# Dealing the late y rows from SBUF with one copy per bank, moves on two queues, and every store on Sync

## The chip, the cores and the metric

The kernel runs on one core of a Trainium2 chip. The metric is the device time of one execution in microseconds (us), as the median of several runs. A ratio is the mean time of one kernel's fast runs over the mean time of the other's fast runs of the same rounds, so it is not quite the ratio of the medians quoted beside it; each ratio comes with a 95% interval. "Faster" or "slower" is said only from 2% on, which is 8.8 us here.

In the profile PE is TensorE's matmul side, DVE is VectorE, ACT is ScalarE, POOL is GpSimd and SP is Sync; "SPq" and "ACTq" are the sequencers of Sync and ScalarE, where transfers are issued. L1005 is line 1005 of the kernel's text.

## The reference, cut to what matters

Attention with a forget gate over `q, k, v, f` of (8, 8, 576, 64) gives `x` of (8, 576, 512). Then a spectral mix is added and a layer closes it:

```python
X = np.fft.rfft(x, axis=1)[:, :64]                 # 64 modes
Y[:, :64] = X * (w_r + 1j * w_i)                   # a 512x512 matrix for each mode
u = x + np.fft.irfft(Y, n=576, axis=1)
out = u + np.maximum(u @ w_ch, 0.0)
```

## The kernel before

The weights of the 64 modes stream in for most of the time. When the last modes are done, their results ("the late y rows", 16 rows of each of the 8 batches) must be put into the tile `yy`, from which the inverse transform reads. They come out of PE in two PSUM banks: `ply` (transposed y, bf16) and `plw` (y times `w_ch`, f32). Batch 0's rows are copied to `yy` directly. The other batches' rows lie in other partitions, so a bank is first emptied into `yl` in SBUF, and then DMA transfers ("moves", 16 KB each) carry them:

```python
y_rows(YTl, 0, ply[:, :], plw[:, :])                                  # PE fills both banks
nc.vector.tensor_copy(row_slot(0, 0, H2, H4), ply[0:H4, :])           # batch 0 straight from PSUM
nc.scalar.copy(yls[0][:, 0, :], ply[:, :])                            # the whole bank, by ScalarE
emit_moves(yls[0], H2, 1, 0, nc.gpsimd)
run(terms(jobs[0], ps, 0, "y"))
nc.vector.tensor_copy(row_slot(0, 1, H2, H4), plw[0:H4, :])
nc.vector.tensor_copy(yls[0][:, 1, :], plw[:, :])
emit_moves(yls[0], H2, 1, 1, nc.gpsimd)
for b in range(2, B):
    for t in range(2):
        emit_moves(yls[0], H2, b, t, nc.gpsimd)
```

Then 20 jobs make the output. Jobs 0 to 3 and 4 belong to batches 0 and 1, jobs 5 to 9 to batches 2 and 3, and so on. In each, PE fills two PSUM tiles: `pu` (u) and `pz` (u @ w_ch). ScalarE copies `pu` to SBUF, VectorE combines `pz` with it, and the result is stored:

```python
def emit_u(job, ps, u, split=False):
    ...
        nc.scalar.copy(u[:, bs, :], ps[0][:, bs, :])

def emit_o(job, ps, u, o, pair, split=False):
    ...
        nc.vector.scalar_tensor_tensor(
            o[:, bs, :], ps[1][:, bs, :], 0.0, u[:, bs, :], ALU.max, ALU.add
        )
        if sb == 4:                                # the last 64 rows of two batches
            for h in range(2):
                eng = nc.scalar if job is jobs[-1] and h else nc.sync
                eng.dma_start(out[b + h, 512:576, :], o[64 * h : 64 * h + 64, 0, :])
        ...                                        # all other stores: nc.sync.dma_start
```

The very last job's output leaves as two half-stores (64 partitions, 128 KB each): one on Sync, one on ScalarE.

The softmax here doesn't subtract the row's maximum and nothing guards it: scores larger than these inputs give would overflow.

## Time and profile before

| | before |
|---|---|
| median of the first three runs | 437.82 us (437.63 to 437.91) |
| profiled span | 435.5 us |
| first `ply` transpose, where the changed code begins | 401.68 us |
| VectorE's last combination ends | 427.82 us |
| last store has landed | 434.2 us |
| ScalarE's queue (q10) | 80 packets, 0.13 MB |
| Pool's issues in the tail | 14 moves |

The table reads as three stretches: 401.7 us that the change does not touch, 26.1 us from the late rows to VectorE's end, and 7.7 us of draining stores and closing. The lines that show the limits of each are in the prediction. The same cut, with all times counted from the start of the `ply` transposes, is used for every kernel below, because the moment at which that start comes differs between the traces by up to 1.8 us (400.5 to 402.2), as the result will show.

### The profile page before, as it was taken

Reading aid. Unit: us, or ns where it says so; the run is one execution under the profiler, and the core shown is the slowest. Engines: PE = TensorE matmul, PEld = TensorE weight load, DVE = VectorE, ACT = ScalarE, POOL = GpSimd, SP = SyncE. Lnnn points to the kernel's source line nnn. Section 1 sums busy time; section 2 is a strip of 40 time slices with the busy share of each in tenths; the row PEclk is TensorE's granted clock in tenths of the full one; section 3 lists DMA queues with packets and bytes.
Section 4 is the critical chain, followed back from the end, with each engine's and each line's share of the span. In section 5 each row is a group of like instructions: output and inputs, shape, how many; then the busy total and the mean of one; then the engine's idle time right before and its main releaser. Section 6 shows DMA issues by size and latency. Waiting matters only on the chain.

```text
span 435.5 us, 12294 instructions
## 1 busy us (share of the span) xinstructions
PE 361.2 (83%) x5295; PEld 245.6 (56%) x5313; DVE 264.0 (61%) x658; ACT 224.8 (52%) x340; POOL 128.6 (30%) x202
## 2 busy tenths in 40 slices
PE   3787799999987977778768797799999978989981
PEld 2353666676665655666556565666665544644440
DVE  5797788876465655546656577524324653743892
ACT  2887488774626356364364554143443442731771
POOL 7333332333233233232333222233223223200600
PEclk9997699996557668557587779599999998989997
DMA  8999999999999999999999999999999999994698
GB/s 182 234 235 240 235 236 239 235 212 237 233 215 237 225 224 237 211 236 230 216 237 212 211 211 211 212 211 211 211 211 211 211 211 211 211 211 97 225 374 293
DMA packets 50981, 97.37 MB, mean 224 GB/s; under 512 B 3792, under 2 KB 12976, under 8 KB 50928
## 3 DMA queue, kind: packets, MB, share of 16 engines
q0 software_dynamic: 46688, 86.16, 100.9%
q1 hardware_dynamic: 4160, 10.31, 6.5%
q8 instruction: 41, 0.67, 0.6%
q10 hardware_dynamic: 80, 0.13, 0.2%
q14 instruction: 12, 0.10, 0.1%
HBM read 163.73 MB, written 9.44 MB: 398 GB/s over the span
## 4 chain that ended last, share of the span: by engine, by line
PE 39%; DMA 23%; ACT 12%; DVE 10%; issue 4%; POOL 0%; DVEq 0%; ACTq 0%
DMA wb<-in_moe_w_i_dram 22%; ACT E L576 8%; PE pav L614 8%; PE A L188 7%; PE ps L569 7%; PE tp L307 5%; PE px L657 3%; DVE QTs L322 2%; PE vp L541 2%; PE pu L828 2%; ACT KT L320 2%; PE pz L828 1%; DVE XT L671 1%; DVE os L1005 1%; DVE E L591 1%
## 5 line engine op out<-in xcount | busy, mean ns | idle before, releaser
L576 ACT ACTIVATE E<-ps 128x1024 bf16<-128x1024 f32 (+1 forms) x128 | 101.5, 851 | 24.0 <-PE ps L569 13.4
L93 POOL DMA_DIRECT2D wb<-in_moe_w_r_dram x64 | 42.5, 664 | 124.8 <-PE A L188 25.0
L188 PE MATMUL A<-XT,wb 128*128 128x16 bf16 x1984 | 69.9, 181 | 10.5 <-DMA wb<-in_moe_w_i_dram 5.7
L188 PEld LDWEIGHTS <-wb 128*128 128x128 bf16 x1984 | 63.4, 100 | 24.9 <-issue 12.1
L569 PE MATMUL ps<-QTs,KT 64*128 64x64 bf16 (+4 forms) x384 | 58.2, 322 | 19.9 <-ACT E L576 17.9
L93 POOL DMA_DIRECT2D wb<-in_moe_w_i_dram x64 | 42.3, 660 | 80.7 <-DMA wb<-in_moe_w_i_dram 36.8
L614 PE MATMUL pav<-va,E 128*128 128x65 bf16 (+1 forms) x1088 | 55.2, 209 | 3.1 <-DVE x_all L636 2.6
L614 PEld LDWEIGHTS <-E 128*128 128x128 bf16 (+1 forms) x1088 | 45.3, 114 | 18.7 <-issue 9.1
L591 DVE TENSOR_TENSOR E<-E,trimask 128x256 bf16<-128x256 bf16 (+2 forms) x128 | 37.0, 303 | 20.3 <-ACT E L576 20.0
L326 ACT COPY VT<-tp 128x640 bf16<-128x640 bf16 (+1 forms) x32 | 23.2, 761 | 34.0 <-PE tp L307 34.0
L867 ACT CAST XW<-pxw 128x512 bf16<-128x512 f32 x36 | 20.7, 586 | 35.7 <-PE pxw L860 23.5
L569 PEld LDWEIGHTS <-KT 64*128 64x128 bf16 x384 | 19.1, 98 | 33.1 <-issue 21.7
L320 ACT COPY KT<-tp 128x640 bf16<-128x640 bf16 (+1 forms) x32 | 22.0, 750 | 26.4 <-PE tp L307 26.2
L910 ACT CAST XW<-pB 128x512 bf16<-128x512 f32 x36 | 20.9, 585 | 28.1 <-PE pB L828 28.0
L860 PE MATMUL pxw<-wch,yy 128*128 128x512 bf16 x133 | 33.6, 385 | 1.2 <-issue 0.7
L909 DVE CAST x_all<-pA 128x512 bf16<-128x512 f32 x36 | 24.9, 692 | 15.2 <-PE pA L828 13.4
L322 DVE COPY QTs<-tp 128x640 bf16<-128x640 bf16 (+1 forms) x32 | 23.3, 768 | 13.9 <-PE tp L307 13.7
L636 DVE TENSOR_TENSOR x_all<-pav,rcp 128x384 bf16<-128x384 f32 x64 | 29.2, 456 | 0.9
L625 DVE RECIPROCAL rcp<-pav 128x6 f32<-128x6 f32 x64 | 12.1, 190 | 24.1 <-PE pav L614 23.4
L153 DVE TENSOR_TENSOR YTe<-A,Yacc 128x128 bf16<-128x128 f32 x16 | 5.9, 368 | 33.1 <-PE A L188 33.1
L828 PEld LDWEIGHTS <-ident_bf 64*64 64x64 bf16 (+1 forms) x348 | 15.7, 109 | 17.6 <-issue 8.8
L541 PE MATMUL vp<-ident_bf,VT 128*128 128x128 bf16 x160 | 17.1, 247 | 5.2 <-DVE QTs L322 4.6
(143 smaller groups left out, 620.0 us busy)
## 6 DMA issues: line engine op xcount, KB each, us to landing
wb<-in_moe_w_r_dram POOLq DMA_DIRECT2D x62, 512.0 KB, 17.0
wb<-in_moe_w_i_dram POOLq DMA_DIRECT2D x62, 512.0 KB, 17.6
stv<-in_v_dram POOLq DMA_DIRECT2D x10, 576.0 KB, 15.2
out_dram<-os SPq DMA_DIRECT2D x10, 512.0 KB, 4.8
stk<-in_k_dram POOLq DMA_DIRECT2D x11, 288.0 KB, 15.2
stq<-in_q_dram POOLq DMA_DIRECT2D x11, 288.0 KB, 15.2
wx<-in_v_dram POOLq DMA_DIRECT2D x5, 576.0 KB, 15.5
out_dram<-uo SPq DMA_DIRECT2D x3, 512.0 KB, 4.3
```

The lines of the kernel that those rows point to most:

```text
L93: keep(nc.gpsimd.dma_start(dst, src))
L188: ins = nc.tensor.matmul(A[:, eb, mi, :], lhsT=w_of(mi, eb * 128), rhs=x_of(m), start=(i == 0), stop=(i == len(terms) - 1),)
L320: nc.scalar.copy(rows(KTs[pr % 2][:, :, 0:S]), tv)
L322: ins = nc.vector.tensor_copy(rows(QT[pr][:, :, :]), tv)
L541: nc.tensor.transpose(vp[:, sc, :, :].rearrange("p b d -> p (b d)"), VTs[s // 2 % 2][:, h, sc * 128 : (sc + 1) * 128], ident_bf[:, :],)
L569: nc.tensor.matmul(ps[:, b, o : o + n], lhsT=KTs[pr % 2][bs, h, jb * 128 : (jb + 1) * 128], rhs=QT[pr][bs, h, jb * 128 + c0 : jb * 128 + c ...
L576: nc.scalar.activation(E[:, :, piece * 512 : piece * 512 + w], ps[:, :, 0:w], ACT.Exp, scale=scale,)
L591: nc.vector.tensor_tensor(dg, dg, tr, ALU.mult)
L614: nc.tensor.matmul(pav[64 * half : 64 * half + w, slot, :], lhsT=E[:, b, c : c + (w - 1) * st + 1 : st], rhs=va[:, jb, b, :], start=(n == ...
L636: nc.vector.tensor_tensor(xo, pi, ri, ALU.mult)
L828: return nc.tensor.matmul(p, lhsT=lhsT, rhs=rhs, start=first, stop=not first, skip_group_check=True)
L860: nc.tensor.matmul(pxw[:, :], lhsT=xT[:, eb, i * 128 : (i + 1) * 128], rhs=wch[:, eb, :], start=(eb == 0), stop=(eb == NDC - 1),)
```

## The change

Its intent: ScalarE is freed of one copy and PSUM of double reading; each late bank is read once, by VectorE, and batch 0 is dealt from SBUF; the moves of batches 1 and 2 go out on Sync, the others on Pool, so that batches 3 and 4 wait less; the last half-store moves from ScalarE to Sync. The diff in full:

```diff
--- before.py
+++ after.py
@@ -821,7 +821,7 @@
         def emit_moves(yl, r0, b, t, eng):
             p0 = H4 * b
             ins = eng.dma_start(row_slot(b, t, r0, H4), yl[p0 : p0 + H4, t, :])
-            if eng is nc.gpsimd:
+            if eng is nc.gpsimd or r0 == H2:
                 tc.keep_in_program_order(ins)
 
         def add(p, lhsT, rhs, first):
@@ -1009,8 +1009,7 @@
                 n_wide = 4 * (b // 2 - 1) + sb
                 if sb == 4:
                     for h in range(2):
-                        eng = nc.scalar if job is jobs[-1] and h else nc.sync
-                        eng.dma_start(
+                        nc.sync.dma_start(
                             out[b + h, 512:576, :], o[64 * h : 64 * h + 64, 0, :]
                         )
                 elif not wide(job):
@@ -1066,14 +1065,18 @@
         ply = ply[:, 0 : D // 2].bitcast(BF16)
         plw = psL.tile([128, D], F32, tag="A", name="plw")
         y_rows(YTl, 0, ply[:, :], plw[:, :])
-        nc.vector.tensor_copy(row_slot(0, 0, H2, H4), ply[0:H4, :])
-        nc.scalar.copy(yls[0][:, 0, :], ply[:, :])
-        emit_moves(yls[0], H2, 1, 0, nc.gpsimd)
+        def late_rows(t, src):
+            keep(nc.vector.tensor_copy(yls[0][:, t, :], src))
+            keep(nc.vector.tensor_copy(row_slot(0, t, H2, H4), yls[0][0:H4, t, :]))
+            for b in (1, 2):
+                emit_moves(yls[0], H2, b, t, nc.sync)
+            for b in (3, 4):
+                emit_moves(yls[0], H2, b, t, nc.gpsimd)
+
+        late_rows(0, ply[:, :])
         run(terms(jobs[0], ps, 0, "y"))
-        nc.vector.tensor_copy(row_slot(0, 1, H2, H4), plw[0:H4, :])
-        nc.vector.tensor_copy(yls[0][:, 1, :], plw[:, :])
-        emit_moves(yls[0], H2, 1, 1, nc.gpsimd)
-        for b in range(2, B):
+        late_rows(1, plw[:, :])
+        for b in range(5, B):
             for t in range(2):
                 emit_moves(yls[0], H2, b, t, nc.gpsimd)
         lctx.close()
```

The pin (`keep_in_program_order`) also covers the moves of Sync. PE's stream is the same in both kernels; only copies, moves and the last store change their place.

## The prediction

> **What bounds the kernel now.** I read the page first, for the stages; then the chain that ended last, for the stretch that the change touches; then the timeline there; last the table by stretches, for what limits the end. From the page:
>
> ```profile
> PE   3787799999987977778768797799999978989981
> ...
> DMA  8999999999999999999999999999999999994698
> GB/s 182 234 235 240 235 236 239 235 212 237 233 215 237 225 224 237 211 236 230 216 237 212 211 211 211 212 211 211 211 211 211 211 211 211 211 211 97 225 374 293
> ```
>
> One slice is 10.9 us. For 36 of 40 slices the DMA engines are full (the weights arrive). The change touches none of that: all its lines run after the last mode tile, so 401 of the 435.5 us stand. Only the last 34 us are in play: first the late y rows are dealt to their places, then 20 jobs are computed (PE fills two PSUM tiles, ScalarE copies one, VectorE combines both) and stored. The chain in order of time, around the dealing:
>
> ```profile
> 401.70 0.38 PE ply L809 x4
> ...
> 404.68 1.43 POOL yy L823 x3
> 406.12 3.42 DMA yy<-yl
> 409.53 0.04 issue
> 409.57 0.40 PE pu L828 x2
> ```
>
> This is the wait that the change is after. Pool issues 14 moves of 16 KB; the fifth is the first half of batch 3, issued at 406.12, landing 3.42 us later, and PE has to hold job 5 (batches 2 and 3) for it. The timeline of the engines (start, us, engine, line, what; in brackets the idle time before and what ended it) shows how much that costs:
>
> ```profile
> 402.12 0.41 DVE L1069 COPY yy<-ply 16x512 bf16<-16x512 bf16 x1 [0.49 <-PE ply L809]
> 402.57 0.58 ACT L1070 COPY yl<-ply 128x512 bf16<-128x512 bf16 x1 [7.46 <-DVE yy L1069]
> ...
> 402.98 0.68 DVE L1073 CAST yy<-plw 16x512 bf16<-16x512 f32 x1 [0.45 <-PE plw L813]
> ...
> 403.70 0.69 DVE L1074 CAST yl<-plw 128x512 bf16<-128x512 f32 x1
> ...
> 404.51 1.29 DVE L1005 SCALAR_TENSOR_TENSOR uo<-pz,uo 128x512 f32<-128x512 f32 x2
> ...
> 404.68 4.77 POOL L823 DMA_DIRECT2D yy<-yl  x10 [0.43 <-DVE yl L1074]
> ...
> 409.57 0.40 PE L828 MATMUL pu<-yy,BIl 64*64 64x512 bf16 x2 [0.39 <-DMA yy<-yl]
> ...
> 410.48 0.69 DVE L1005 SCALAR_TENSOR_TENSOR uo<-pz,uo 128x512 f32<-128x512 f32 x1 [0.40 <-PE pz L828]
> ```
>
> PE loses 0.39 us to the move, and VectorE then 0.40 us before job 4 at 410.48, where its other breaks are about 0.2 us. So the wait on show is small. The last view is the busy time by stretches:
>
> ```profile
> 410.00:414.00 4.00, 3.73 (x59) 2.04 (x58) 3.57 (x5) 3.57 (x4) 1.04 (x3) 1.00 0.93 336
> 414.00:418.00 4.00, 3.63 (x59) 1.91 (x54) 3.64 (x4) 3.00 (x5) 0.00 (x0) 1.00 1.02 383
> ...
> 422.00:426.00 4.00, 3.54 (x56) 1.75 (x49) 3.60 (x4) 2.94 (x3) 0.00 (x0) 1.00 1.03 405
> 426.00:430.00 4.00, 0.69 (x6) 0.13 (x3) 1.83 (x3) 0.58 (x1) 0.00 (x0) 0.95 1.01 387
> ```
>
> The last two numbers of a line are the DMA share and GB/s. VectorE is busy 3.6 of each 4 us, and from 414 on the DMA engines are full with stores. The tail is bound by both; VectorE ends at 427.82, the last store lands at about 434.2. An earlier start of the jobs moves both; a wait removed that is shorter than VectorE's own work moves nothing.
>
> **What the Trainium skill says.** "PSUM — Partial Sum Buffer", Terms: two engines may not be at the same bank and quadrants at once, reads included. The trace agrees: ScalarE's copy of ply starts at 402.57, 0.04 us after VectorE's copy from the same bank ends (402.12 + 0.41). "VectorE: DVE Perf Modes", The perf-mode tier table: a bf16 copy runs at up to 4x from SBUF, at most 2x from PSUM. The trace agrees: 128x512 bf16 from PSUM took 416 ns (0.81 ns per element), 128x1152 bf16 from SBUF 461 ns (0.40). "DMA: Bandwidth & Descriptors", Issuing engines are not separate DMA queues: transfers from all issuers share the 16 DMA engines, so another issuer saves only issue time. The trace agrees so far as one queue, Sync's, alone fills them from 414 to 429.
>
> **The change part by part.**
>
> (1) VectorE's work. Before: 16x512 from PSUM (0.41), 16x512 cast (0.68), 128x512 cast (0.69): 1.78 us. After: 128x512 bf16 from PSUM (0.42, as the like copy of yl from yp), 128x512 cast (0.69), and two 16x512 copies within SBUF. For these the nearest rows are 64x640 at 0.32 and 128x64 at 0.26, so I estimate 0.30 each. Sum 1.71: the same. ScalarE loses one copy of 0.58, while it was otherwise waiting for PE (its next copy starts at 403.54 on PE's word), so nothing is won there.
>
> (2) When batch 0 can go on. Its first half was in place at 402.53, now at 402.53 + 0.04 + 0.30 = 402.87. PE is in the plw matmuls until 402.87 anyway: cost under 0.1. Its second half was in place at 403.66; now 402.98 + 0.69 + 0.30 = 403.97, so 0.3 later. The last matmuls of job 0 started at 403.72 right on that copy, so VectorE's first combination slips from 404.51 to about 404.8. Against that, the plw bank is read for the last time at 403.67 instead of 404.39, and job 1's second PSUM tile, which reuses it, waited until 404.44 for that. PE may thus do job 1 as early as before, and VectorE, which stood 0.22 us idle before job 1, reaches it at 406.0 to 406.1 against 406.02. Net +0.05 for jobs 1 to 3.
>
> (3) The moves. On Sync, batches 1 and 2, first half: ready 402.53, issued at 402.6 and 403.2 (0.59 each in the trace), second half at 403.7 and 404.3, done by 405. Sync's earlier moves end at 401.23 and its first store begins at 405.23, so the stores do not queue behind them. Pool: batch 3 at about 402.9 instead of 406.12, and 403.9 for its other half. With 3.5 us to land, the median of both queues, batch 3 is in place at 406.4 and 407.4, some 2 us before PE asks at 409.0. The wait of 0.39 goes wholly. VectorE's job 4 then starts at 410.1 to 410.2 instead of 410.48, job 5 at about 410.85 instead of 411.09 (it also needs a PSUM tile free from job 3, which ends at 410.1). Gain 0.25 after the 0.05 of part 2.
>
> (4) The moves also leave the DMA engines before 410 rather than at 413.6. Pool's queue took 5.5% of the engines from 400 to 420, which is 1.1 us for 14 moves, 0.08 us each; the four or so that fell after 410 are 0.3 us of work in the nearly full stretch. But stores were still limited by VectorE there; I count nothing.
>
> (5) The last stores. Before, one half went out on ScalarE at 427.86 and landed in 4.8 us; the other on Sync at 428.99, because Sync was held to 428.90 by the store ahead, took 1.42 to issue and landed 5.2 us later, at 434.2: it sets the end. Now both are on Sync, so the second is issued at about 430.4 less what is gained. The earlier pair of such stores, at 422.97 and 424.16, landed 0.33 apart, the second 4.0 us after its issue. So: the first lands 0.3 us sooner, as 128 KB less (0.3 us at 405 GB/s) share the engines, the second 0.33 after it, at 434.2 to 434.4. Cost 0.05.
>
> Sum: -0.25 (parts 2 and 3) + 0.05 (part 5) = -0.2 us. 437.82 - 0.2 = 437.6.
>
> **The rivals.** First, *the end becomes an issue chain on Sync*. If the second half-store lands 4.7 us after its issue (the median of all half-stores) and not 4.0, the end is 435.1, 0.9 us later, and the gain of part 3 only takes it back to +0.65: 438.5. For it speaks that Sync's half-stores took 1.1 to 1.6 us to issue under load; against it, that the engines are full until 433.3, so the second store's bytes queue behind others anyhow. Second, *the start binds*: the 0.3 us by which batch 0's second half is late runs through PE, VectorE and all jobs, with the bank's early release worth nothing since job 1's next matmuls also wait for a ScalarE copy ending at 404.61. That makes part 3 only cancel it: 437.9. Third, *the moves were worth more than the one wait shows*: the tail's jobs close up, the store stream starts full 0.5 us sooner, and the end follows: 437.2. Fourth, *the dealt rows are hidden anyway*: the DMA engines bound the end whatever VectorE does, and the time does not move, 437.8.
>
> **Range and chances.** Every path stays within 1 us, and 2% is 8.8 us; even all 34 us of the tail would have to shrink by a quarter. The three runs before span 0.28 us, so another build adds 0.2 or so. Predicted 437.6 us, range 437.0 to 438.3. Faster by over 2%: 0.01; within 2%: 0.98; slower by over 2%: 0.01.
>
> **What would show it.** Part 1: two 16x512 copies within SBUF near 0.30 us; a row near 0.4 or more makes part 2 worse. Part 2: VectorE's first combination at about 404.8 and job 1 near 406.0; if job 1 starts at 406.3, the second rival holds. Part 3: no wait of PE for a move, batch 3 issued by Pool near 402.9, and job 4 on VectorE by 410.2. Part 5: the interval between the last two landings, and the time from VectorE's end to the end of the span, 7.7 us before. It would be wrong if the compiled order of the matmuls around job 0 and 1 changed, if Pool took over a microsecond to wake, or if Sync's moves were slowed so that the first stores start after 405.6.

## The result, and the profile after

| | before | after |
|---|---|---|
| median, 6 runs each | 437.73 us (437.27 to 438.17) | 436.77 us (435.82 to 437.33) |
| ratio | | 0.9975, 95% interval 0.9961 to 0.9988 |
| profiled span | 435.5 us | 435.2 us |

"Same" at 2%, as foreseen, but the gain is 0.96 us and not 0.2, and the median lies 0.23 us below the predicted range. All outputs are right. The page after, its two rows on the DMA engines, 40 slices of the span:

```profile
DMA  8999999999999999999999999999999999995797
GB/s 184 234 235 241 234 236 238 235 212 236 234 215 236 225 224 237 210 238 233 214 237 211 212 211 212 211 211 211 211 211 211 212 210 211 211 211 100 253 367 274
```

They answer to the rows that the prediction shows: full until the tail, then a dip while the rows are dealt, then stores. Nothing there tells 1 us. VectorE around the dealing, after (start, us, engine, line, what; in brackets the idle time before it and what ended it):

```profile
401.35 0.42 DVE L1069 COPY yl<-ply 128x512 bf16<-128x512 bf16 x1 [0.49 <-PE ply L809]
401.81 0.28 DVE L1070 COPY yy<-yl 16x512 bf16<-16x512 bf16 x1
402.21 0.69 DVE L1069 CAST yl<-plw 128x512 bf16<-128x512 f32 x1
402.94 0.29 DVE L1070 COPY yy<-yl 16x512 bf16<-16x512 bf16 x1
403.99 2.52 DVE L1005 SCALAR_TENSOR_TENSOR uo<-pz,uo 128x512 f32<-128x512 f32 x3 [0.77 <-DMA yy<-yl]
...
410.48 1.23 DVE L1005 SCALAR_TENSOR_TENSOR os<-pz,us 128x1024 f32<-128x1024 f32 x1 [0.54 <-issue]
```

The small copies take 0.28 and 0.29 us. The moves go out as planned; Sync's and Pool's issues in the same kernel:

```profile
401.80 2.41 SPq L823 DMA_DIRECT2D yy<-yl  x4
```

```profile
402.47 4.81 POOL L823 DMA_DIRECT2D yy<-yl  x10 [17.17 <-DVE yy L1070]
```

The chain of waits after no longer holds a move: it runs from the last weights through PE to VectorE's jobs (with one store among them, from 416.86 to 420.50), and no piece of Pool is in it.

Two profiles can't be subtracted as they stand. The `ply` transposes start at 401.68 us before and at 400.91 after, 0.77 us apart, though no line ahead of them has changed. The stretch from 384 to 390 us shows where this comes from (busy time of PE, its weight loads, VectorE, ScalarE and Pool, then the granted clock, which is the share of TensorE's full clock that the chip allowed, the DMA share and GB/s), first before, then after:

```profile
384.00:390.00 6.00, 5.56 (x59) 2.92 (x60) 2.22 (x4) 1.42 (x3) 0.53 (x1) 0.72 1.12 211
```

```profile
384.00:390.00 6.00, 6.00 (x84) 3.31 (x79) 3.78 (x7) 2.91 (x6) 0.53 (x1) 0.97 1.12 211
```

The granted clock was 0.72 here in one execution and 0.97 in the other. A second profile of the kernel before and one with the last store undone had 0.72 too, the others 0.97 to 1.00. The chain of waits shows what came with it. Before, where the chain stays on PE ahead of `ply`:

```profile
400.01 0.29 PE A L172 x8
400.30 0.33 PE pu L828 x2
...
401.07 0.29 PE A L172 x8
...
401.70 0.38 PE ply L809 x4
```

After, where PE waits for the last weights:

```profile
384.77 15.42 DMA wb<-in_moe_w_i_dram
400.19 0.04 issue
400.23 0.36 PE A L172 x8
...
400.93 0.38 PE ply L809 x4
```

In the eleven traces with 0.97 to 1.00, `ply` starts 0.72 or 0.73 us after the last weights have landed; in the three with 0.72, 1.71 to 1.79 us after it. So the low clock comes with 1.0 us, which is more than the gain. (In this pair the last weights also landed 0.22 us later after the change, which leaves the 0.77.) All three traces with the low clock have the halves of the last store on two queues, as before: three of five such traces, and none of the nine others. No edit touches anything ahead of `ply`, so chance is the nearest reading, but no run tests it: for the timed runs the record has the clock of the whole span only. The timed ratios have to carry the argument, and the aligned stretches have to be read with care.

Aligned, the kernels stand so (us):

| stretch | before | after |
|---|---|---|
| `ply` start to VectorE's end | 26.14 | 26.23 |
| VectorE's end to the last landing | 6.38 | 6.24 |
| last landing to the end of the span | 1.31 | 1.82 |
| sum | 33.83 | 34.29 |

That is a puzzle: in this pair of profiles the changed tail is 0.46 us longer, while the timed runs are 0.96 us shorter. One trace is one execution, and these two took 437.23 and 436.95 us, only 0.28 us apart. So each part was undone or done alone, and timed in several rounds.

### The profile page after: what moved, and what is told of

It is laid out like the page before. It is cut to its first block, busy times and chain, and to the rows that moved or that the text cites. A ratio compares the mean times of both kernels' runs of the same rounds, so it can differ in the third digit from the quotient of the medians.

```text
span 435.2 us, 12314 instructions
## 1 busy us (share of the span) xinstructions
PE 368.1 (85%) x5313; PEld 249.7 (57%) x5313; DVE 263.7 (61%) x659; ACT 224.4 (52%) x339; POOL 126.8 (29%) x198
## 4 chain that ended last, share of the span: by engine, by line
PE 35%; DMA 26%; ACT 12%; DVE 10%; issue 4%; SPq 0%; DVEq 0%; POOL 0%; ACTq 0%
DMA wb<-in_moe_w_i_dram 25%; ACT E L576 8%; PE pav L614 7%; PE ps L569 7%; PE A L188 6%; PE tp L307 5%; PE px L657 2%; PE vp L541 2%; DVE QTs L322 2%; ACT KT L320 2%; ACT VT L326 2%; DVE XT L671 1%; DVE os L1005 1%; DVE E L591 1%; PE px L682 1%
## 5 line engine op out<-in xcount | busy, mean ns | idle before, releaser
L569 PE MATMUL ps<-QTs,KT 64*128 64x64 bf16 (+4 forms) x384 | 60.2, 334 | 16.6 <-ACT E L576 14.7
L614 PE MATMUL pav<-va,E 128*128 128x65 bf16 (+1 forms) x1088 | 57.1, 214 | 3.2 <-DVE x_all L636 2.6
L614 PEld LDWEIGHTS <-E 128*128 128x128 bf16 (+1 forms) x1088 | 47.0, 118 | 16.9 <-issue 7.0
L860 PE MATMUL pxw<-wch,yy 128*128 128x512 bf16 x144 | 36.0, 388 | 0.0
L541 PE MATMUL vp<-ident_bf,VT 128*128 128x128 bf16 x160 | 18.4, 261 | 4.6 <-DVE QTs L322 3.9
```

What stands on the lines that cost most here:

```text
L541: nc.tensor.transpose(vp[:, sc, :, :].rearrange("p b d -> p (b d)"), VTs[s // 2 % 2][:, h, sc * 128 : (sc + 1) * 128], ident_bf[:, :],)
L569: nc.tensor.matmul(ps[:, b, o : o + n], lhsT=KTs[pr % 2][bs, h, jb * 128 : (jb + 1) * 128], rhs=QT[pr][bs, h, jb * 128 + c0 : jb * 128 + c ...
L614: nc.tensor.matmul(pav[64 * half : 64 * half + w, slot, :], lhsT=E[:, b, c : c + (w - 1) * st + 1 : st], rhs=va[:, jb, b, :], start=(n == ...
L860: nc.tensor.matmul(pxw[:, :], lhsT=xT[:, eb, i * 128 : (i + 1) * 128], rhs=wch[:, eb, :], start=(eb == 0), stop=(eb == NDC - 1),)
```

## The experiments

The theories, in short. The *move theory*: the gain is the move wait that is gone. The *store theory*: the gain is that the last half-store left ScalarE. The *copy theory*: one reader for each bank. And the *chance theory*: a build's place or the clock, nothing of the three. The expectations use letters for them; those that matter later are C1 (the two halves should follow each other in one queue, whichever), C2 (a second queue that takes turns with Sync's slows the DMA engines), its two forms C2a and C2b, and E (an end sequence that grows with Sync's transfers).

All traces in one table, cut as above (us). "Last stores" is the disputed part: the queues that they are issued from. The column of 2 KB packets is the mean time that a 2 KB packet took after VectorE's end, worked out from the packet records of the traces.

| run | moves | last stores | VectorE's end | to last landing | to end | 2 KB packet, ns | ratio (95%) |
|---|---|---|---|---|---|---|---|
| before | Pool | halves split | 26.14 | 6.38 | 1.31 | 123 | 1 |
| before_again | Pool | split | 26.18 | 6.49 | 1.32 | 123 | 0.9996 (0.9980 to 1.0012) |
| only_copies | Pool | split | 26.23 | 6.58 | 1.31 | 126 | 1.0003 (0.9991 to 1.0015) |
| only_moves | both | split | 26.10 | 7.08 | 1.83 | 117 | 1.0015 (0.9995 to 1.0034) |
| undo_stores | both | split | 26.23 | 6.46 | 1.83 | 120 | 0.9992 (0.9973 to 1.0011) |
| act_both | Pool | both halves ScalarE | 26.65 | 6.10 | 1.16 | 137 | 1.0002 (0.9988 to 1.0016) |
| act_both_again | Pool | both halves ScalarE | 26.73 | 6.60 | 1.16 | 133 | 0.9991 (0.9973 to 1.0008) |
| full_on_act | both | one full store ScalarE | 26.23 | 6.13 | 1.83 | 104 | 1.0015 (0.9993 to 1.0037) |
| only_stores | Pool | all Sync | 26.79 | 5.94 | 1.14 | 102 | 0.9988 (0.9976 to 1.0001) |
| only_stores_again | Pool | all Sync | 26.27 | 5.78 | 1.15 | 108 | 0.9974 (0.9956 to 0.9992) |
| after | both | all Sync | 26.23 | 6.24 | 1.82 | 109 | 0.9975 (0.9961 to 0.9988) |
| after_again | both | all Sync | 26.22 | 6.55 | 1.81 | 107 | 0.9985 (0.9973 to 0.9997) |
| after_third | both | all Sync | 26.23 | 5.64 | 1.82 | 103 | 0.9980 (0.9962 to 0.9997) |
| sem_back | both | all Sync | 26.23 | 6.04 | 1.56 | 104 | 0.9990 (0.9976 to 1.0004) |

### The changed kernel again, and each part alone

**after_again** is the changed kernel without an edit, in five rounds.

> The changed kernel once more. In the two profiles the stretch from the first matmul of ply to the end is 33.8 us before and 34.3 after, so the changed kernel's tail is no shorter; what is shorter there, by 0.8 us, lies ahead of ply, in code that is the same, where the granted clock from 384 to 396 was 0.86 before and 0.98 after. Theory A (clock): most of the 0.96 us between the medians is the clock that the runs happened to be granted; then this repeat gives a ratio nearer to 1, 0.9985 to 1.0005, and the time follows the listed clock. Rival B (the change): the gain is real, ratio 0.9965 to 0.9985 again.

Measured: 436.34 us, before 437.07 us, ratio 0.9985. The gain is there again, 0.73 us by the medians; the ratio lies on the edge of both ranges.

**only_stores** is the kernel before with the last store's edit alone:

```diff
-                        eng = nc.scalar if job is jobs[-1] and h else nc.sync
-                        eng.dma_start(
+                        nc.sync.dma_start(
```

> The kernel before with one part of the change: the last store's second half goes out on Sync, not ScalarE. Theory A: nothing, ratio 0.9995 to 1.001, the last landing within 0.2 us of 32.5 us after ply. Rival C (the last stores carry the gain): ratio 0.9965 to 0.9985 and a last landing at least 0.5 us sooner. Rival D (the second store queues behind the first on Sync): 1.001 to 1.002.

Measured: 436.38 us, ratio 0.9988, interval 0.9976 to 1.0001. This one edit gives as much as the whole change, within the intervals. But the ratio lies between the ranges of A and C, and the last landing was not half a microsecond sooner, as C had it: it came 32.73 us after `ply`, against 32.52 before. In this execution job 4 started late (9.45 us after `ply`); in the repetition below the last landing came at 32.05.

**only_moves** keeps the copies and stores of before and takes the new order and queues of the moves, with their pin:

```diff
-        emit_moves(yls[0], H2, 1, 0, nc.gpsimd)
+        for bb, eng in ((1, nc.sync), (2, nc.sync), (3, nc.gpsimd), (4, nc.gpsimd)):
+            emit_moves(yls[0], H2, bb, 0, eng)
```

(and the same for the second bank).

> The kernel before with its copies and stores, but the moves in the changed order and on the changed queues. Theory A: PE's wait for batch 3's move goes and VectorE reaches job 4 about 0.4 us sooner after ply (8.4 for 8.8), but the end follows by 0 to 0.3 us: ratio 0.9990 to 1.0005. Rival B: this is the part that gains, ratio 0.9965 to 0.9985.

Measured: 437.35 us, ratio 1.0015: no gain. Its trace shows why, and it is the clearest of all for this, since nothing else in it has changed. First PE, ScalarE and VectorE of only_moves from job 3 to job 6:

```profile
409.03 0.37 PE L828 MATMUL pz<-x_all,ident_bf 64*64 64x512 bf16 x1 [0.70 <-DVE uo L1005]
```

```profile
410.15 1.93 ACT L1000 COPY us<-pu 128x1024 f32<-128x1024 f32 x2 [0.99 <-PE pu L828]
```

```profile
407.75 1.82 DVE L1005 SCALAR_TENSOR_TENSOR uo<-pz,uo 128x1024 f32<-128x1024 f32 x2 [0.19 <-PE pz L828]
409.76 1.23 DVE L1005 SCALAR_TENSOR_TENSOR os<-pz,us 128x1024 f32<-128x1024 f32 x1 [0.18 <-issue]
411.19 1.23 DVE L1005 SCALAR_TENSOR_TENSOR os<-pz,us 128x1024 f32<-128x1024 f32 x1 [0.21 <-ACT us L1000]
```

Follow the releasers back from the last line. Job 6 waits for ScalarE's copy; that copy waits for PE; and PE, at 409.03, waits for VectorE: for job 3's combination, 407.75 to 408.98, to give back its PSUM tile. From there it takes 0.05 + 1.12 us to ScalarE's start and 1.04 us more to job 6: 2.21 us. In the kernel before the same chain is 2.24 us long (job 3 ends at 410.09, job 6 starts at 412.33), and job 3 starts 7.17 us after `ply` in both. So the move wait of before, real as it was, stood beside a chain that was nearly as long. With it gone, job 4 comes 0.49 us sooner (8.31 instead of 8.80 us after `ply`), job 5 0.23 us, and job 6 0.04 us.

**only_copies** lets VectorE empty both banks and deal batch 0 from SBUF, with all moves on Pool in the old order:

```diff
-        nc.vector.tensor_copy(row_slot(0, 0, H2, H4), ply[0:H4, :])
-        nc.scalar.copy(yls[0][:, 0, :], ply[:, :])
+        keep(nc.vector.tensor_copy(yls[0][:, t, :], src))
+        keep(nc.vector.tensor_copy(row_slot(0, t, H2, H4), yls[0][0:H4, t, :]))
```

> The kernel before with its moves on Pool and its stores, but VectorE empties both banks and deals the first batch from SBUF. Theory A: VectorE's first combination 0.2 to 0.3 us later after ply (3.1 for 2.83), the later ones within 0.1: ratio 0.9995 to 1.001. Rival B: with ScalarE freed and the plw bank given back 0.7 us sooner, 0.9965 to 0.9985.

Measured: 437.3 us, ratio 1.0003. The copies are worth nothing in either direction.

### A control, and the stores undone and repeated

**before_again** is the kernel before, built and run as an experiment, to see what a build without any edit does.

> The kernel before against itself, a control for the noise of the comparison and a second trace. Both theories: ratio 1.000, within 0.0010 either way. Theory C (the last stores carry the gain) expects this trace's last landing 32.5 to 33.0 us after ply and its total, with the clock full from 384 to 396, at 435.2 to 435.6. Theory A (clock) expects a total of 434.4 if the clock is full there.

Measured: 437.23 us, ratio 0.9996, interval 0.9980 to 1.0012. Another build alone gives nothing that can be told from none. The last landing, 32.67 us after `ply`, is as theory C had it; the total decides nothing, because the clock was low again.

**undo_stores** is the changed kernel with only the last half-store back on ScalarE (the edit of only_stores the other way round).

> The changed kernel with the last half-store back on ScalarE. Theory C: the gain goes, ratio 0.9995 to 1.0010. Rival B (moves and copies together carry it, though neither did alone): 0.9970 to 0.9988. Theory A (clock): 0.9990 to 1.0010 as well, but then the run of the stores alone, sent beside it, does not repeat its 0.9988 either.

Measured: 437.33 us, ratio 0.9992, between the two ranges, with an interval that holds 1 (0.9973 to 1.0011). **only_stores_again** repeats the single edit.

> The run of the stores alone once more, with undo of the same part beside it. Theory C: 0.9975 to 0.9992 again. Theory A: 0.9995 to 1.0005.

Measured: 436.06 us, ratio 0.9974, interval 0.9956 to 0.9992. So the edit was put in twice, with 0.9988 and 0.9974, and taken out once, which left nothing that can be told from no gain. Taken over all runs: the six with every store on Sync have ratios from 0.9974 to 0.9990, 0.9982 in the mean; the four with the halves split (before_again, only_copies, only_moves, undo_stores) from 0.9992 to 1.0015, 1.0002 in the mean. No one of the first lies above any of the second. The difference, 0.0020 of 437 us, is about 0.85 us.

The landings say what one would see of it. The two last half-stores before, on Sync and on ScalarE (time from issue to landing), then after, both on Sync:

```profile
DMA to landing us min/median/max: 4.8/5.0/5.2
```

```profile
DMA to landing us min/median/max: 3.9/4.4/4.8
```

And the DMA engines, from two microseconds after VectorE's end on, in steps of 1 us (the last two numbers are the DMA share and GB/s). Before:

```profile
429.82:430.82 1.00, 0.00 (x0) 0.00 (x0) 0.00 (x0) 0.00 (x0) 0.00 (x0) 0.50 1.01 373
430.82:431.82 1.00, 0.00 (x0) 0.00 (x0) 0.00 (x0) 0.00 (x0) 0.00 (x0) 0.50 0.99 270
431.82:432.82 1.00, 0.00 (x0) 0.00 (x0) 0.00 (x0) 0.00 (x0) 0.00 (x0) 0.50 1.03 375
432.82:433.82 1.00, 0.00 (x0) 0.00 (x0) 0.00 (x0) 0.00 (x0) 0.00 (x0) 0.50 0.40 150
```

After:

```profile
429.14:430.14 1.00, 0.00 (x0) 0.00 (x0) 0.00 (x0) 0.00 (x0) 0.00 (x0) 0.50 1.03 414
430.14:431.14 1.00, 0.00 (x0) 0.00 (x0) 0.00 (x0) 0.00 (x0) 0.00 (x0) 0.50 1.02 410
431.14:432.14 1.00, 0.00 (x0) 0.00 (x0) 0.00 (x0) 0.00 (x0) 0.00 (x0) 0.50 0.97 272
432.14:433.14 1.00, 0.00 (x0) 0.00 (x0) 0.00 (x0) 0.00 (x0) 0.00 (x0) 0.50 0.22 80
```

In both the engines are full (a share of about 1), and in both one line falls to about 270 GB/s. That is where the 2 KB packets of the half-stores are moved: 16 engines that take 123 ns for each 2 KB move 266 GB/s, and with 168 ns for each 4 KB they move 390. So the low line by itself is no loss. It comes earlier before, where ScalarE's half-store takes turns with the full store ahead of it, than after, where both halves go last. What is lost can be read from the single packets. With the halves split, a 2 KB packet took 122 ns and a 4 KB packet 169 ns in the mean of five traces; with every store on Sync 105 and 165 ns in the mean of six. For the 128 packets of 2 KB and some 420 of 4 KB, spread over 16 engines, that makes 0.24 us (an estimate from these four numbers, unrounded). The prediction did not think of this: it took the share of 1.02 for the limit and counted bytes, as if a byte cost the same in either arrangement.

Over all traces with the halves split, VectorE's end to the last landing is 6.60 us in the mean of five; with every store on Sync it is 6.03 us in the mean of six. The spread inside a group is wide (6.38 to 7.08, and 5.64 to 6.55), and not all of the 0.57 us is the last store's doing. At VectorE's end, before the last half-store is issued, the packets still to come hold 2.08 MB in the mean of the first group and 1.97 MB in that of the second. These 27 packets of 4 KB more are 0.28 us; the slower packets are the 0.24.

Nor do the traces put the whole gain here. The mean spans of the two groups are 435.71 and 434.78 us, 0.93 apart. Of that, 0.55 us lie ahead of `ply` (401.41 against 400.86), where no edit reaches and where three traces of the first group had the low clock; from `ply` to the last landing the difference is 0.41 us (32.77 against 32.36). So the timed runs show that the gain comes with the last store's queue, and the traces locate about 0.24 us of it. Where the rest falls, and whether the low clock has to do with the edit, stays open.

"DMA: Bandwidth & Descriptors", Queues, rings and completion order, says that each engine goes round between the queue rows that it has work for, packet by packet. The trace before agrees: the half-store on ScalarE, issued 0.16 us after the last full store on Sync, landed 1.24 us ahead of it (30.96 against 32.20 us after `ply`). What the page does not say is that the packets then take longer: while the turns lasted, ScalarE's 2 KB packets took 162 ns each, and those of the other half, which came last on Sync, 85.

### What about the queue: act_both, act_both_again, full_on_act

Theories C1 and C2 differ on one arrangement: both halves next to each other, but in ScalarE's queue. **act_both** is the kernel before with

```diff
-                        eng = nc.scalar if job is jobs[-1] and h else nc.sync
+                        eng = nc.scalar if job is jobs[-1] else nc.sync
```

> The kernel before with both halves of the last store on ScalarE. Theory C1 (the two halves should follow one another in one queue; apart, the last one moves its 64 partitions alone): the last landing 0.3 us sooner after VectorE's end than before (6.1 to 6.3 us for 6.4 to 6.5), ratio 0.9978 to 0.9992. Theory C2 (a second queue taking turns with Sync's stores is what costs): last landing as before or later, ratio 0.9995 to 1.0010.

Measured: 437.59 us, ratio 1.0002, as C2 had it; the 2 KB packets took 137 ns; but the last landing came 6.10 us after VectorE's end, as C1 had it. A second time, **act_both_again**:

> The kernel before, with both halves of the last job's store on ScalarE, a second time, now in 5 rounds of its own. Theory C1 (it matters only that the two halves follow each other in one queue): ratio 0.9978 to 0.9992, VectorE's end to the last landing 5.7 to 6.2 us. Theory C2 (the halves take turns with Sync's full stores, and that slows the engines): ratio 0.9995 to 1.001, 6.3 us or more, and packets of 2 KB at 120 to 140 ns (137 in the first trace) instead of 102 to 109.

Measured: 436.52 us, before 437.01 us, ratio 0.9991, interval 0.9973 to 1.0008; 2 KB packets 133 ns, VectorE's end to the last landing 6.60 us. The drain of that trace:

```profile
429.78:430.78 1.00, 0.00 (x0) 0.00 (x0) 0.00 (x0) 0.00 (x0) 0.00 (x0) 0.50 1.02 342
430.78:431.78 1.00, 0.00 (x0) 0.00 (x0) 0.00 (x0) 0.00 (x0) 0.00 (x0) 0.50 0.96 268
431.78:432.78 1.00, 0.00 (x0) 0.00 (x0) 0.00 (x0) 0.00 (x0) 0.00 (x0) 0.50 0.99 369
```

The low line stands ahead of the full store's end, as before, and the packets are slow in both traces, which speaks for C2. The last landings do not decide (6.10 and 6.60), and the second ratio would still allow a part of C1 (its interval reaches down to 0.9973). So C1 is not supported, and not refuted either.

**full_on_act** asks whether any store on a second queue does it, or only a half-store. It is the changed kernel with the second full store of the last wide pair on ScalarE:

```diff
-                        nc.sync.dma_start(
+                        eng = nc.scalar if job is jobs[-2] and j else nc.sync
+                        eng.dma_start(
```

> The changed kernel, with the second full store of the last wide pair (512 KB, 128 partitions) issued by ScalarE; both halves of the last job stay on Sync. Theory C2a (any second queue that takes turns with Sync's slows the engines while the last stores drain): from VectorE's end to the last landing 6.4 to 6.7 us, as in the five traces with the half-store on ScalarE, instead of the 6.0 of the six traces with all on Sync; ratio to the kernel before 0.9995 to 1.001. Theory C2b (only the half-store of 64 partitions in turns with a full one costs it): 5.8 to 6.2 us, ratio 0.9975 to 0.999.

Measured: 437.47 us, before 437.01 us, ratio 1.0015, interval 0.9993 to 1.0037. By the time, the gain is gone, as C2a has it. By the trace it is not: 6.13 us, 2 KB packets 104 ns, and the low line comes only where both halves go last:

```profile
428.79:429.79 1.00, 0.00 (x0) 0.00 (x0) 0.00 (x0) 0.00 (x0) 0.00 (x0) 0.61 1.01 406
429.79:430.79 1.00, 0.00 (x0) 0.00 (x0) 0.00 (x0) 0.00 (x0) 0.00 (x0) 0.50 1.08 426
430.79:431.79 1.00, 0.00 (x0) 0.00 (x0) 0.00 (x0) 0.00 (x0) 0.00 (x0) 0.50 0.96 287
```

as C2b has it. Neither form is borne out by both. What the times of all seven experiments with a store on ScalarE have in common is that none of them shows a gain that its interval would hold up; the slow 2 KB packets come with the half-stores alone. So the times show that taking the last store off ScalarE's queue gives the gain. Slower packets are shown for the half-stores, and they are worth 0.24 us by the working above. The rest has no cause that a run shows: it may be that a second queue in use at all (the kernel before uses ScalarE's for this one store only) costs something that no drain shows, and it may be that the low clock ahead of `ply` comes more often with it. That stays open.

### The end of the program: sem_back

In every trace with the new moves, but that of the run below, 1.8 us pass from the last landing to the end, against 1.3 us before. Sync's waits in that stretch are on other engines' sequencers (us in all, times, longest), before and after:

```profile
SPq L1138 <- PEq L1138: 0.3, 2, 0.2
```

```profile
SPq L1141 <- PEq L1141: 0.7, 2, 0.5
```

Theory E: four more transfers on Sync lengthen its closing sequence. **sem_back** is the changed kernel with four of the earlier moves, those of batches 0 and 1, put on Pool, which brings the count of Sync's moves back:

```diff
-                            emit_moves(yls[1], H2 + H4, b, t, nc.sync)
+                            emit_moves(yls[1], H2 + H4, b, t, nc.gpsimd if b < 2 else nc.sync)
```

> The changed kernel, but four of the sixteen earlier moves of y rows (batches 0 and 1, some 10 us ahead of the late ones and waited for by nothing near) go out on Pool, which is idle then. So Sync and ScalarE issue as many transfers as before the change. Theory E: the last store's semaphore is one of a ring of eight that Sync waits for in a fixed order at the end; the four extra moves on Sync turned the ring so that the last store comes first in that order and the rest follows after it, 1.8 us from the last landing to the end in both traces of the changed kernel against 1.3 before. Here then 1.1 to 1.3 us, the tail 0.5 us shorter than the changed kernel's, ratio 0.9960 to 0.9978 against the kernel before. Rival F (the longer end comes with the moves on Sync themselves or with what Sync has to fetch): still 1.8 us, ratio as the changed kernel's, 0.9975 to 0.9988.

Measured: 437.12 us, before 437.35 us, ratio 0.9990; last landing to the end 1.56 us. Neither range was met: half of the 0.5 us is back in the trace, and the time shows no gain beyond the changed kernel's. The instruction records say which half. Sync ends with a fixed row of semaphore waits. The one that the last landing ends is followed by seven more in the changed kernel, and by three in sem_back and in the kernel before, some 0.07 us apart: this part is theory E's, and it came back, 0.26 us. The rest is one pause of 0.45 us between two of these waits, in sem_back as in the changed kernel, and not before; its cause stays open, as rival F's part. (sem_back's six runs also took 1.9 us outside the profiled span, where the kernel before took 1.7; no trace shows why.) **after_third**, the changed kernel in the same rounds:

> The changed kernel beside the two, for a comparison on one chip: ratio 0.9975 to 0.9990, 1.8 us from the last landing to the end.

Measured: 436.55 us, ratio 0.9980, and 1.82 us from the last landing to the end, both as expected. So the 0.5 us that the profile shows at the end is not found in the times: kernels with the new moves and every store on Sync (0.9975, 0.9985, 0.9980) do as well as those with the old moves (0.9988, 0.9974). The profiled execution of each experiment is one of its timed runs, so the stretch is not the profile's own. The moves may gain elsewhere what it costs (with every store on Sync, VectorE's end came at 26.79 and 26.27 us with the old moves and at 26.22 or 26.23 with the new), or the spread of the runs hides it; no run settles it. It also solves no more than half of the puzzle above. Of the 0.46 us by which the profiled tail after was longer, 0.51 is this stretch; but the timed gain of 0.96 us has then only 0.05 us in that pair of tails to answer to it. Executions differ by more than that: the drain of the changed kernel was 6.24, 6.55 and 5.64 us in three profiles.

No version tried beats the changed kernel. The single edit of the stores does as well.

## Why the prediction was wrong

"Within 2%" was right and the size was not: -0.2 us were predicted, about -0.9 us came (0.96 and 0.73 by the medians of the first two comparisons; 0.9980 in the mean of three ratios). By its own steps:

- **Part 1 held.** The two small copies were estimated at 0.30 us each and took 0.28 and 0.29.
- **Part 2 held.** VectorE's first combination was to come 0.3 us later and job 1 about 0.05: they came 0.25 (3.08 against 2.83 us after `ply`) and 0.03 (4.37 against 4.34). That refutes the second rival, a late start that runs through. The line of VectorE's first combination names a move as the last releaser, but job 0 needs only rows that VectorE itself wrote; a label of that kind is the semaphore that came last, not the cause.
- **Part 3 was right about the wait and wrong about its worth.** PE waits for no move any more, and job 4 starts 8.35 us after `ply` instead of 8.80; on the clock of before this is 410.03, even ahead of the predicted 410.1 to 410.2. But "Gain 0.25 after the 0.05 of part 2" did not reach job 6, which starts at 10.71 instead of 10.65: the chain from job 3's PSUM tile over PE and ScalarE, 2.21 us, was there all the time, and only_moves shows it with nothing else changed. The prediction named that tile itself ("it also needs a PSUM tile free from job 3") and did not follow it to the end. The term measured: 0. In the changed kernel job 5 even starts 0.15 us later than before (9.56 against 9.41); VectorE stood idle for 0.54 us before it, with no releaser named. The delay comes with the new copies: job 5 starts at 9.56 or 9.57 in all seven traces that have them, only_copies among them, and at 9.18 in only_moves, which is the predicted 410.85 on the clock of before. What it waits for is not shown.
- **What part 3 is good for is the late move.** In the six other traces with the old order of moves, job 4 started between 8.59 and 9.45 us after `ply`; where it was late (9.45, 9.31 and 9.40 in only_stores, act_both and act_both_again), the delay passed to the end whole, VectorE's end being 26.79, 26.65 and 26.73. In all traces with the new moves it is 26.10 to 26.23. The times do not tell this apart from nothing.
- **Part 4 held**, so far as can be seen: nothing was counted for it, and only_moves shows no gain.
- **Part 5 failed, and it is the step that made the number wrong.** "The first lands 0.3 us sooner [...], the second 0.33 after it, at 434.2 to 434.4. Cost 0.05." The second half-store did land 0.3 us after the first (4.8 us after issue for the first, 3.9 for the second, issued 1.2 us later), so the picture of two stores in a row was right. What failed is what it was compared with: the prediction priced the half on ScalarE's queue as free, so that moving it to Sync could only cost. Instead of +0.05 the term measured about -0.85 us by the timed runs. The slower packets while two queues are at work account for 0.24 us of it by the traces; the cause of the rest stays open. With -0.85, and job 6 at +0.06 in place of the -0.25 of parts 2 and 3, the sum is -0.8 us, near the -0.9 measured; that is no independent check, since the -0.85 comes from the same kind of runs.
- **The rivals.** The first (an issue chain on Sync that costs 0.65 us) was refuted: Sync did issue the second half 1.2 us after the first, but it landed 3.9 us after its issue and not 4.7 (3.5 to 4.2 in all six traces with every store on Sync). The third named -0.6 us and came nearest in size, by luck: its reason, that the jobs close up, is refuted by only_moves. The fourth, that the dealt rows are hidden, has the number that only_moves and only_copies measured for their parts, but not the reason: it let the DMA engines bind whatever VectorE does, and VectorE's end itself hardly moved (26.10 and 26.23 against 26.14 us).
- **The range** was too narrow for another reason as well. It was drawn from three runs of one kernel within 0.28 us; the runs of that same kernel in the later sets spread over 0.8 to 3.0 us, and the medians of the sets lie between 437.0 and 437.7.

The prediction also leaned on "DMA: Bandwidth & Descriptors", Issuing engines are not separate DMA queues: another issuer is said to save only issue time. Read with care this holds, and no more follows; the prediction went on to treat the second queue as free, and the timed runs show a cost.

## What to carry to other kernels

Before you price a wait that the profile shows, follow the chain of buffers past it to the next engine: a wait of 0.39 us stood beside a chain of PE and ScalarE that was as long, and taking it away moved the end by nothing. Where the DMA engines are full at the very end of a kernel, try all last stores in one queue before you spread them over two; here it was worth some 0.2%, as much as the whole change. And align two traces at the first instruction that the change touches, and repeat them, before you subtract anything: here that instruction came 1.0 us later after the last weights wherever the granted clock had been low.

## What the Trainium skill lacked or had wrong

- "DMA: Bandwidth & Descriptors", Issuing engines are not separate DMA queues, says that a second issuer saves only issue time. It lacks that it can cost: with one or both 128 KB half-stores on ScalarE beside Sync's last stores, 2 KB packets took 117 to 137 ns instead of 102 to 109, and with one of them there the kernel took about 0.85 us longer, of which the slower packets explain 0.24. (With one full store on ScalarE the gain was gone as well, without slower 2 KB packets: 104 ns.)
- The same page, Queues, rings and completion order, gives the turns between queue rows but not their price for a mix of 2 KB and 4 KB packets; here 4 KB packets took 167 to 171 ns with two queues of halves and full stores, and 164 to 165 ns with one.
- "Runtime: NRT & Kernel Launch", The ~15µs preamble/postamble breakdown, gives about 1.5 us for the closing barrier. Whether the stretch here is the same one no run shows, but in the profiles it is not fixed: from the last landing to the end 1.14 to 1.83 us passed, 0.26 us of it by the place that the last store's wait has in Sync's closing row, while the times did not follow.
